# K by two transfers of 64 partitions instead of four of 32, from the ninth pack on

## The chip, the cores and the metric

The kernel runs on one NeuronCore of a Trainium2 chip. The metric is the device time of one execution in microseconds (us). Five instruction streams take part: PE (TensorE, matrix products; its weight loads are shown apart as PEld), DVE (VectorE), ACT (ScalarE), POOL (GpSimd) and SP (SyncE, which here does nothing but issue transfers). Sixteen DMA engines move the data between the device's memory and the core's on-chip memory; the transfers issued by SP go through one queue (q1 in the profile), those issued by ACT through another (q10).

## The reference

Two independent attention blocks, A and B, each with a cache of keys and values, joined along the last axis. The inputs are bfloat16 and seeded random numbers times 0.1.

```python
B, Sq, D = 16, 64, 640
H, Sk, Dh = 32, 512, 128          # k_cache, v_cache: (B, H, Sk, Dh), 64 MB each

def block(x, k_cache, v_cache, wq, wo):
    q = (x @ wq).reshape(B, Sq, H, Dh).transpose(0, 2, 1, 3)
    scores = einsum("bhqd,bhkd->bhqk", q, k_cache) * Dh ** -0.5
    p = softmax(scores, axis=-1)
    o = einsum("bhqk,bhkd->bhqd", p, v_cache)
    return o.transpose(0, 2, 1, 3).reshape(B, Sq, H * Dh) @ wo

out = concatenate([block(A...), block(B...)], axis=-1)     # (16, 64, 1280)
```

Each cache is read once. The caches are 268 MB of the 292 MB that the profile says are read.

## The kernel before, in words

**Packs.** The work is cut into 128 packs. A pack is two batches and four heads of one block; four packs (`NJ`) are a group, eight groups a phase, and there are four phases (block A heads 0-15, A 16-31, B 0-15, B 16-31). Between phases the projection weights are replaced. For a pack the kernel

- projects q for its heads (PE, `em_QP`, L611; ACT copies it out of PSUM, L617),
- turns K in 32x32 blocks (DVE, `em_KT`, L625, two instructions),
- forms the scores (PE, `em_S`, L635), takes exp with the row sums (ACT, L654), the reciprocals (DVE, L667), and multiplies (POOL, L683),
- transposes the probabilities (PE, L694; DVE copies, L704), multiplies by V (PE, `em_PV`, L717) and by the output weights (PE, `em_OP`, L737).

**Loads.** A pack needs 1 MiB of K and 1 MiB of V. `em_LDV` (L563) brings V as two transfers, one for each batch, of 128 partitions with 4 KB in each. `em_LDK` (L556) brings K as four transfers of 32 partitions with 8 KB in each. In K's tile `kn_ring` a partition is 4 * (head and eighth of the sequence) + 2 * (batch) + (half): the transfer `(n, i)` with `b = i // 2` and `l = i % 2` fills every fourth partition from `2 * b + l` on, and reads 32 pieces of 8 KB that lie 16 KB apart in the cache. The other half (`l`) is the pieces between; the other batch lies 4 MiB further on.

**Rings.** K has six buffers (`NK`), V four (`NV`). A transfer into a buffer is issued once its last reader is done: for V that is the product with V four packs earlier, on which SP waits (L571). K's transfers need no wait of their own, because SP has by then waited for something later.

**Order.** Nothing is scheduled while the kernel runs. `build_plan` (L60) gives each operation a time in units of packs (`AT`), sorts each engine's program by it, and works out from the tiles that are read and written which semaphore values have to be waited for. SP's program is the list `loads`, sorted by a due time and a class: K of a pack is due `KLEAD` = 2.5 packs ahead of V of the same pack, so that SP's queue reads: V of pack n, K of pack n + 2 or 3, V of pack n + 1, and so on, with x and the weights in between. SP's queue is taken in that order.

**Semaphores of the loads.** Each K buffer has a semaphore (`sem_key`, L268), which every finished transfer moves on. Transfers of one pack can finish in any order, so a reader waits until all of the pack are there: `PARTS` (L18) says that four make up a pack of K, and `wait_count` (L360) rounds a count up to a multiple of it; `Clocks.finish` (L341) does the same in the plan's bookkeeping of what is known to be done. The transposes L625 are the only readers of `kn_ring`. In the trace each transfer leaves, besides its data, one packet of 4 bytes on each of the 16 DMA engines, which moves the semaphore.

Of the kernel before, what the change touches and what calls it, by code (L numbers as in the profile page):

```python
# [14 lines left out]
SUM_MAX = 2.0 ** 40  # L15


PARTS = dict(d_v=2, d_k=4)  # L18


class Cfg:
    NK = 6
# [7 lines left out]
    PERIOD = 4  # L30
    BASE = 32
    KLEAD = 2.5
    NARROW = 2
    AT = dict(XT=-2.585, XE=-2.383, XC=-0.788, QP=-0.428, QE=-0.224, KT=(-0.672, -0.65), S=0,
              EX=(0.307, 0.252, 0.358, 0.4), RC=(0.45, 0.6), RCO=0.48, NM=(0.803, 0.854, 1.088, 1.187),
# [2 lines left out]


class Op:  # L40
    __slots__ = ("eng", "kind", "idx", "reads", "writes", "sem", "count", "deps", "waits", "ts", "dma")

    def __init__(self, eng, kind, idx, ts, reads=(), writes=()):
        self.eng = eng
        self.kind = kind
        self.idx = idx
        self.reads = tuple(reads)
        self.writes = tuple(writes)
        self.sem = None
        self.count = None  # L50
        self.deps = []
        self.waits = []
        self.ts = ts
        self.dma = kind in ("LDK", "LDV", "LDX", "LDWQ", "LDWO", "ST")


# [3 lines left out]
def build_plan(dims, cfg, general):  # L60
# [7 lines left out]
    AT = cfg.AT  # L68
    ops = []
    loads = []  # L70
    at = {}

    def add(eng, kind, idx, ts, reads=(), writes=()):
        op = Op(eng, kind, idx, ts, reads, writes)
        ops.append(op)
        at[(kind, idx)] = op
        return op

    def add_output(n):
# [12 lines left out]
        add("act", "OE", (n, 0), n + AT["OE"][0], [], [("B", 4), ("B", 5), ("oT", 0)])  # L92
        add("act", "OE", (n, 1), n + AT["OE"][1], [], [("B67",), ("oT", 1)])
        add("act", "ZO", n, n + AT["ZO"], [("zeros",)], [("B67",)])
        add("pe", "OP", n, n + AT["OP"], [("oT", 0), ("oT", 1), ("wo", j)], [("B67",)])
        if j == NJ - 1:
            bp = g % NBP
            add("dve", "OS", g, n + AT["OS"], [("acc", bp)], [("B67",), ("out_sb",) if final else ("acc", bp)])
            if final:
                add("act", "ST", g, n + AT["ST"], [("out_sb",)], [("out_dram", g)])  # L100
# [17 lines left out]
    for ph in range(NPH):  # L118
        twp = [ph * PH + j + (AT["WP1"] if ph else AT["WP0"]) for j in range(NJ)]
        for kt in range(dims["KT"] if ph else 0):  # L120
            ready = twp[-1] - PH + 0.5 if ph > 1 else NJ - 1 + AT["WP0"] + 0.5
            op = add("sp", "LDWQ", (ph, kt), twp[0] - 0.5, [], [("ws", kt, j) for j in range(NJ)])
# [17 lines left out]
    for n in range(-2, N):  # L140
        add_output(n)
        if n < 0:
            continue
        g, j = n // NJ, n % NJ
        add("pe", "QP", n, n + AT["QP"], [("xT", g % cfg.NX), ("wqp", j)], [("SB", 1)])
        add("act", "QE", n, n + AT["QE"], [], [("SB", 1), ("qs", n % cfg.NQ)])
        for i in range(4):
            op = add("sp", "LDK", (n, i), n + AT["KT"][0] - 0.9, [], [("kn", n % cfg.NK)])
            loads.append((n - cfg.NV + AT["PV"] + 0.2 - cfg.KLEAD, 2, op))
        for b in range(2):  # L150
            tk = n + AT["KT"][b]
            add("dve", "KT", (n, b), tk, [("kn", n % cfg.NK)], [("kt", n % cfg.NKT, b)])
        add("pe", "S", n, n + AT["S"], [("qs", n % cfg.NQ), ("kt", n % cfg.NKT, 0), ("kt", n % cfg.NKT, 1)],
            [("SB", i) for i in range(4)])
        for i in range(4):
            h = 4 * n + i
            te = n + AT["EX"][i]
            if general:
                add("dve", "MX", h, te - 0.002, [], [("SB", i), ("negmax", h % 4)])
            add("act", "EX", h, te, [("negmax", h % 4)] if general else [],  # L160
                [("SB", i), ("p", h % cfg.NP), ("rs", h)])
            add("pool" if n < N - 1 else "dve", "NM", h, n + (AT["NM"] if n < N - 1 else AT["NMZ"])[i], [("p", h % cfg.NP), ("recip", n % cfg.NR, i // 2)], [("pn", i)])
        for a in range(2):
            add("dve", "RC", (n, a), n + (AT["RCO"] if n % NJ == 1 and not a else AT["RC"][a]), [("rs", 4 * n + i) for i in (2 * a, 2 * a + 1)],
                [("recip", n % cfg.NR, a)])
# [10 lines left out]
    for op in sorted(ops, key=lambda o: o.ts):  # L176
        deps = []
# [22 lines left out]
    for k in range(reps):  # L200
        for i in range(size):
            o, o0 = pe[lo + k * size + i], pe[lo + i]
# [76 lines left out]
    for eng in ENGINES:  # L279
        for op in progs[eng]:  # L280
            op.sem = sem_key(op)
            counts[op.sem] = op.count = counts.get(op.sem, 0) + 1
    need = {}
    for op in ops:
        need[id(op)] = [e for e in (stand_in(d, op) for d in op.deps) if e is not None and e is not op]
# [39 lines left out]
class Clocks:  # L325
# [15 lines left out]
    def finish(self, eng, op):  # L341
        ck = self.clock[eng]
        self.val[op.sem] = self.val.get(op.sem, 0) + 1
        c2 = dict(ck)
        if op.dma:
            c2[op.sem] = op.count
        else:
            self.own[eng][op.sem] = op.count
            for s2, v2 in self.own[eng].items():
                if c2.get(s2, 0) < v2:  # L350
                    c2[s2] = v2
        part = PARTS.get(op.sem[0], 1)
        for k in range(op.count - 1, (op.count - 1) // part * part, -1):
            for s2, v2 in self.snap[(op.sem, k)].items():
                if c2.get(s2, 0) < v2:
                    c2[s2] = v2
        self.snap[(op.sem, op.count)] = c2


def wait_count(d):  # L360
    part = PARTS.get(d.sem[0], 1)
    return -(-d.count // part) * part


def order_waits(progs, need, base):
# [68 lines left out]
def mha_kernel(nc, blocks, out, cfg=None):  # L434
    cfg = cfg or Cfg()
# [4 lines left out]
    KT = D // 128  # L440
# [10 lines left out]
    def wide(n):  # L451
        return n < NPACK - cfg.NARROW

# [5 lines left out]
    NK, NV, NKT, NX, NXN, NQ, NP, NR = (cfg.NK, cfg.NV, cfg.NKT, cfg.NX, cfg.NXN, cfg.NQ, cfg.NP, cfg.NR)  # L459

    with contextlib.ExitStack() as es:
# [8 lines left out]
        kn_ring = sb("kn_ring", [128, NK, 2, 2048], BF16)  # L470
# [85 lines left out]
        def em_LDK(e, op):  # L556
            n, b, l = op.idx[0], op.idx[1] // 2, op.idx[1] % 2
            blk, bp, j, h = pack_info(n)
            src = blocks[blk][1][2 * bp + b, h:h + 4].rearrange("h (p l t) d -> l (h p) (t d)", l=2, t=32)[l]
            ins = e.dma_start(kn_ring[2 * b + l::4, n % NK].rearrange("p a c -> p (a c)"), src)  # L560
            return ins, ins

        def em_LDV(e, op):  # L563
# [361 lines left out]
```

## Time and profile before

| | |
|---|---|
| time, median of 3 runs | 740.34 us (740.29 to 740.70) |
| profiled execution: time / span | 740.13 us / 738.40 us |
| granted TensorE clock | 0.994 |
| PE busy | 679.2 us (92%) |
| DVE / ACT / POOL busy | 526.1 / 529.1 / 404.0 us |
| moved by DMA | 295.15 MB in 79837 packets, mean 400 GB/s |
| K transfers | 512 of 256 KB |
| V transfers | 256 of 512 KB |

The span is the time from the first to the last instruction; the profiled execution's own time is 1.73 us more, and lies 0.21 us under the median. A row of a group of instructions names the line, the engine, the operation, what is written from what, and then busy time, mean time of one, and the idle time of the engine just before them with what ended most of it. In the chain of work that ended last, an engine's name with a q (SPq) is its instruction queue: for SP that is the time that issuing a transfer took, which includes waiting until the queue has room. Rows by stage give the busy microseconds and the number of instructions of each engine in a stretch of the span, the granted clock, the mean share of the 16 DMA engines' time that packets took, and the rate. That share can exceed 1, because the records of two packets on one engine overlap slightly.

### The profile page before, as it was taken

What the parts mean: (1) busy time and instruction counts of PE and PEld (TensorE: products, weight loads), DVE (VectorE), ACT (ScalarE), POOL (GpSimd) and SP (SyncE); (2) the same over time, 40 slices, a digit from 0 to 9 for tenths busy, and PEclk for the clock granted to TensorE, in tenths of its full rate; (3) what the DMA queues carried; (4) which work ended last, traced back from release to release, by engine and by line L of the source; (5) the groups of instructions that cost most, each with busy time, mean ns of one, the idle gap of its engine ahead of it and who ended that gap; (6) DMA issues with size and microseconds to landing.
All of it is one profiled execution on the core that took longest, in us unless ns stands there. A gap on an engine that the chain in (4) does not pass through costs nothing.

```text
span 738.4 us, 61575 instructions
## 1 busy us (share of the span) xinstructions
PE 679.2 (92%) x28502; PEld 534.4 (72%) x28502; DVE 526.1 (71%) x818; ACT 529.1 (72%) x1559; POOL 404.0 (55%) x580
## 2 busy tenths in 40 slices
PE   3679999999998999989987989999999799999997
PEld 2458787787776777777766767777777577878785
DVE  7447787777757767777665677667686578788784
ACT  1448888888776767767766777777777577777775
POOL 3635555555964455554683644555577455555461
PEclk9999999999999999999999999999999999999999
DMA  9999999999999999999999999999999999999991
GB/s 323 392 404 414 415 414 414 414 414 415 409 403 413 416 416 415 416 415 415 415 402 407 414 413 415 413 414 413 416 414 402 410 415 415 416 416 417 415 371 36
DMA packets 79837, 295.15 MB, mean 400 GB/s; under 512 B 13360, under 2 KB 28208, under 8 KB 63408
## 3 DMA queue, kind: packets, MB, share of 16 engines
q1 hardware_dynamic: 68384, 281.43, 94.3%
q10 hardware_dynamic: 11408, 13.27, 5.1%
q14 instruction: 35, 0.29, 0.1%
q8 instruction: 10, 0.16, 0.1%
HBM read 292.03 MB, written 2.62 MB: 399 GB/s over the span
## 4 chain that ended last, share of the span: by engine, by line
PE 42%; SPq 40%; DMA 9%; issue 4%; POOL 2%; DVE 2%; ACT 1%; ACTq 0%; POOLq 0%; DVEq 0%
SPq L560 26%; SPq L571 12%; PE ps L717 10%; PE ps L737 10%; PE ps L611 9%; PE ps L635 8%; PE ps L694 5%; DMA kn_ring<-in_B_k_cache_dram 5%; DMA kn_ring<-in_A_k_cache_dram 2%; DMA ws_sb<-in_A_wq_dram 2%; SPq L545 1%; POOL pn_sb L683 1%; POOL wqp_sb L583 1%; DVE kt_ring L625 1%; DVE pT_sb L704 1%
## 5 line engine op out<-in xcount | busy, mean ns | idle before, releaser
L683 POOL TENSOR_SCALAR pn_sb<-p_ring,recip 128x512 bf16<-128x512 bf16 x508 | 341.8, 692 | 304.4 <-DVE recip L667 304.2
L625 DVE STREAM_TRANSPOSE kt_ring<-kn_ring 128x1024 f32<-128x1024 f32 x256 | 302.8, 1222 | 107.8 <-DMA kn_ring<-in_B_k_cache_dram 70.0
L654 ACT ACTIVATE p_ring<-ps 128x512 bf16<-128x512 f32 x512 | 297.8, 596 | 9.3 <-PE ps L635 5.6
L704 DVE COPY pT_sb<-ps 128x1024 bf16<-128x1024 bf16 x258 | 170.7, 673 | 59.9 <-PE ps L694 59.4
L717 PE MATMUL ps<-pT_sb,v_ring 32*128 32x64 bf16 x16512 | 168.0, 192 | 31.9 <-DVE pT_sb L704 17.4
L717 PEld LDWEIGHTS ps<-pT_sb,v_ring 32*128 32x128 bf16 x16512 | 151.5, 91 | 48.7 <-issue 24.8
L725 ACT ACTIVATE oT_sb<-ps 128x256 bf16<-128x256 f32 x260 | 85.6, 381 | 127.0 <-PE ps L717 127.0
L611 PE MATMUL ps<-xT_ring,wqp_sb 128*128 128x128 bf16 x2560 | 165.8, 220 | 7.3 <-POOL xT_ring L600 7.3
L611 PEld LDWEIGHTS ps<-xT_ring,wqp_sb 128*128 128x128 bf16 x2560 | 157.5, 114 | 13.6 <-issue 7.5
L737 PE MATMUL ps<-wo_sb,oT_sb 128*128 128x320 bf16 x1040 | 165.0, 302 | 1.2 <-ACT ps L729 1.2
L635 PE MATMUL ps<-kt_ring,qs_ring 32*64 32x512 bf16 x4096 | 139.7, 382 | 3.8 <-issue 3.8
L737 PEld LDWEIGHTS ps<-wo_sb,oT_sb 128*128 128x128 bf16 x1040 | 91.5, 98 | 38.2 <-ACT ps L729 1.5
L617 ACT ACTIVATE qs_ring<-ps 128x512 bf16<-128x512 f32 x128 | 76.4, 597 | 57.2 <-PE ps L611 56.5
L694 PEld LDWEIGHTS ps<-ident,pn_sb 64*128 64x128 bf16 x4128 | 68.2, 95 | 62.1 <-ACT oT_sb L725 51.9
L654 ACT ACTIVATION_READ_ACCUMULATOR p_ring<-ps 128x1 f32 x512 | 105.6, 206 | 0.0
L694 PE MATMUL ps<-ident,pn_sb 64*128 64x64 bf16 x4128 | 83.3, 191 | 8.0 <-issue 4.1
L635 PEld LDWEIGHTS ps<-kt_ring,qs_ring 32*64 32x64 bf16 x4096 | 55.2, 103 | 31.2 <-issue 5.0
L667 DVE RECIPROCAL recip<-rowsum 128x2 f32<-128x2 f32 x256 | 40.8, 159 | 37.7 <-ACT p_ring L654 29.5
L729 ACT ACTIVATE ps<-zeros 128x256 f32<-128x256 bf16 x130 | 50.4, 388 | 4.2
L583 POOL COPY wqp_sb<-ws_sb 128x1280 bf16<-128x1280 bf16 x32 | 39.2, 1254 | 15.6 <-DMA ws_sb<-in_A_wq_dram 15.6
L600 POOL COPY xT_ring<-xs_sb 128x640 bf16<-128x640 bf16 x32 | 22.9, 716 | 0.4 <-PE ps L611 0.4
L590 PE MATMUL ps<-ident,xn_ring 128*128 128x128 bf16 x165 | 14.9, 222 | 3.8 <-DMA xn_ring<-in_A_x_dram 3.2
(26 smaller groups left out, 66.0 us busy)
## 6 DMA issues: line engine op xcount, KB each, us to landing
kn_ring<-in_A_k_cache_dram SPq DMA_DIRECT2D x256, 256.0 KB
v_ring<-in_A_v_cache_dram SPq DMA_DIRECT2D x128, 512.0 KB, 14.6
kn_ring<-in_B_k_cache_dram SPq DMA_DIRECT2D x256, 256.0 KB
v_ring<-in_B_v_cache_dram SPq DMA_DIRECT2D x128, 512.0 KB, 15.5
ws_sb<-in_B_wq_dram SPq DMA_DIRECT2D x10, 512.0 KB, 16.8
wo_sb<-in_B_wo_dram ACTq DMA_DIRECT2D x8, 640.0 KB, 14.7
ws_sb<-in_A_wq_dram ACTq DMA_DIRECT2D x4, 640.0 KB, 17.7
wo_sb<-in_A_wo_dram SPq DMA_DIRECT2D x4, 640.0 KB, 14.1
```

Source lines behind the costliest of these rows:

```text
L560: ins = e.dma_start(kn_ring[2 * b + l::4, n % NK].rearrange("p a c -> p (a c)"), src)
L571: ins = e.dma_start(dst.rearrange("p t d -> p (t d)"), src.rearrange("h (p t) d -> (h p) (t d)", t=16))
L611: last = e.matmul(ps[:, 1, f * 128:(f + 1) * 128], w[:, kt, f, :], xT_ring[:, xs, kt, :], start=(kt == 0), stop=(kt == KT - 1))
L625: ins = e.transpose(dst.rearrange("p c b (h l) -> p c h b l", h=8, l=2), src)
L635: last = e.matmul(ps[64 * b:64 * b + 64, i, :], qs_ring[rows, n % NQ, f, b, :], kt_ring[rows, n % NKT, :, f // 2, b, :, f % 2], start=(f = ...
L654: ins = e.activation(dst, src, ACTF.Exp, scale=1.0, accum_out=rowsum[:, h:h + 1])
L683: ins = e.tensor_scalar(dst, src, recip[:, h // 4 % NR, i:i + 1], 1.0, ALU.mult, ALU.mult)
L694: last = e.transpose(pt_bank(b)[:, 64 * c:64 * c + 64], pn_sb[rows, c, :], ident[rows, rows], tile_position=(64 * b, 0))
L704: ins = e.tensor_copy(pT_sb[:, b].rearrange("p t q -> p (t q)"), pt_bank(b))
L717: last = e.matmul(ps[:, 4 + i, 64 * b:64 * b + 64], v_ring[rows, n % NV, b, c, :], pT_sb[rows, b, c, :], start=(t == 0 and i < 2), stop=(t ...
L725: ins = e.activation(oT_sb[:, 2 * a:2 * a + 2, :], o_ps[:, 2 * a:2 * a + 2, :], ACTF.Copy)
L737: last = e.matmul(out_ps[:, s, :], oT_sb[:, i, :], wo_sb[:, 4 * j + i, s * NH0:(s + 1) * NH0], start=(j == 0 and i == 0), stop=(j == NJ - ...
```

## The change

Packs 0 to 7 keep four K transfers. From pack 8 on there are two: transfer `l` fills every second partition from `l` on (64 partitions, 8 KB in each), and its source runs over both batches inside each piece (32 pieces, 2 batches, 4096 elements). As packs no longer have the same number of transfers, `PARTS` can't say how many make up one; each K transfer now carries the list of its pack's transfers (`group`), and the two helpers take the smallest and the largest count from that list. The transposes wait, as before, for all transfers of their pack. The order of the programs of PE, DVE, ACT and POOL and the semaphores that they wait on are the same; SP's program is the same but for 240 transfers fewer (two in each of 120 packs).

```diff
-PARTS = dict(d_v=2, d_k=4)
+PARTS = dict(d_v=2)

 class Cfg:
     KLEAD = 2.5
+    KSPLIT = 8

 # build_plan
         for i in range(4):
-            op = add("sp", "LDK", (n, i), n + AT["KT"][0] - 0.9, [], [("kn", n % cfg.NK)])
-            loads.append((n - cfg.NV + AT["PV"] + 0.2 - cfg.KLEAD, 2, op))
+            if i < 2 or n < cfg.KSPLIT:
+                op = add("sp", "LDK", (n, i), n + AT["KT"][0] - 0.9, [], [("kn", n % cfg.NK)])
+                loads.append((n - cfg.NV + AT["PV"] + 0.2 - cfg.KLEAD, 2, op))
...
+    packs = {}
+    for op in ops:
+        if op.kind == "LDK":
+            packs.setdefault(op.idx[0], []).append(op)
+            op.group = packs[op.idx[0]]

 # Clocks.finish
-        part = PARTS.get(op.sem[0], 1)
-        for k in range(op.count - 1, (op.count - 1) // part * part, -1):
+        for k in range(op.count - 1, group_start(op), -1):

+def group_start(d):
+    part = PARTS.get(d.sem[0], 1)
+    return min(o.count for o in d.group) - 1 if d.group else (d.count - 1) // part * part

 def wait_count(d):
     part = PARTS.get(d.sem[0], 1)
-    return -(-d.count // part) * part
+    return max(o.count for o in d.group) if d.group else -(-d.count // part) * part

 # em_LDK
-            src = blocks[blk][1][2 * bp + b, h:h + 4].rearrange("h (p l t) d -> l (h p) (t d)", l=2, t=32)[l]
-            ins = e.dma_start(kn_ring[2 * b + l::4, n % NK].rearrange("p a c -> p (a c)"), src)
+            src = blocks[blk][1][2 * bp:2 * bp + 2, h:h + 4].rearrange("b h (p l t) d -> l (h p) b (t d)", l=2, t=32)[l]
+            if n < cfg.KSPLIT:
+                ins = e.dma_start(kn_ring[2 * b + l::4, n % NK].rearrange("p a c -> p (a c)"), src[:, b])
+            else:
+                ins = e.dma_start(kn_ring[l::2, n % NK].rearrange("p a c -> p (a c)"), src)
```

More of the change, by code (lines that the diff above doesn't have):

```diff
@@ L40 @@
 class Op:
-    __slots__ = ("eng", "kind", "idx", "reads", "writes", "sem", "count", "deps", "waits", "ts", "dma")
+    __slots__ = ("eng", "kind", "idx", "reads", "writes", "sem", "count", "deps", "waits", "ts", "dma", "group")
     def __init__(self, eng, kind, idx, ts, reads=(), writes=()):
@@ L53, in __init__ @@
         self.ts = ts
+        self.group = None
         self.dma = kind in ("LDK", "LDV", "LDX", "LDWQ", "LDWO", "ST")
```

## The prediction, made before the changed kernel was run

> **What bounds the kernel now.** I read the page's totals first, then the rows by stage, then the chain around the last place where a transfer stands in it, and last the trace's single packet records.
>
> ```profile
> span 738.4 us, 61575 instructions
> PE 679.2 (92%) x28502; PEld 534.4 (72%) x28502; DVE 526.1 (71%) x818; ACT 529.1 (72%) x1559; POOL 404.0 (55%) x580
> ...
> DMA  9999999999999999999999999999999999999991
> ...
> DMA packets 79837, 295.15 MB, mean 400 GB/s; under 512 B 13360, under 2 KB 28208, under 8 KB 63408
> ...
> q1 hardware_dynamic: 68384, 281.43, 94.3%
> q10 hardware_dynamic: 11408, 13.27, 5.1%
> ...
> PE 42%; SPq 40%; DMA 9%; issue 4%; POOL 2%; DVE 2%; ACT 1%; ACTq 0%; POOLq 0%; DVEq 0%
> ```
>
> PE and the DMA engines are both nearly full. The chain gives 40% to SP's queue, which looks as if issuing transfers were the limit; the rows by stage say otherwise.
>
> ```profile
> core 0: us, PE busy (x) PEld busy (x) DVE busy (x) ACT busy (x) POOL busy (x), PEclk, DMA share, GB/s
> 60.00:200.00 140.00, 139.48 (x6027) 110.11 (x6012) 109.94 (x171) 114.63 (x337) 83.28 (x121) 1.00 1.02 414
> 200.00:400.00 200.00, 185.73 (x7771) 146.52 (x7768) 140.17 (x222) 143.44 (x427) 113.34 (x161) 1.00 1.03 412
> 400.00:590.00 190.00, 175.25 (x7486) 138.18 (x7488) 131.45 (x210) 137.64 (x406) 106.14 (x152) 1.00 1.02 413
> 590.00:712.00 122.00, 121.73 (x5119) 96.21 (x5112) 96.59 (x148) 94.27 (x281) 65.90 (x99) 1.00 1.02 415
> 712.00:738.00 26.00, 20.89 (x843) 15.98 (x840) 15.62 (x32) 15.04 (x46) 8.04 (x12) 0.96 0.32 121
> ```
>
> The DMA engines are full up to 712 us. PE is full from 60 to 200 us and from 590 to 712 us, but between, it stands idle for 14.27 + 14.75 = 29.0 us. So the middle is bound by the DMA engines; before and after it PE sets the pace, with the DMA engines only just keeping up. What PE lacks in the middle is K:
>
> ```profile
> DVE kt_ring L625 <- DMA kn_ring<-in_B_k_cache_dram: 70.0, 53, 3.8
> DVE kt_ring L625 <- DMA kn_ring<-in_A_k_cache_dram: 37.6, 30, 3.0
> ...
> 569.75 18.86 DMA kn_ring<-in_B_k_cache_dram
> 588.61 0.02 issue
> 588.64 2.37 DVE kt_ring L625 x2
> ```
>
> The last two transposes that the chain reaches through a transfer start at 588.64 us; they are those of pack 102 (the 205th and 206th). From there the chain to the end is PE and its evacuations. So the kernel ends sooner by what the transfers up to K of pack 102 gain; what later ones gain, PE hides.
>
> **What a transfer costs a DMA engine.** SP issues 802 transfers and ACT 33; 835 x 16 = 13360, exactly the packets under 512 B: each transfer ends in one 4-byte packet per engine. The packet records of q1 give its length: median 9 ns, against 313 ns for an 8 KB packet (K) and 160 ns for a 4 KB packet (V). The records also tell what it costs. Over 100 to 180 us, where one data packet follows another directly its record starts 3 or 4 ns (mean 3.6) before the earlier one ends; where a 4-byte packet lies between, it starts 2 or 3 ns (mean 2.4) after. So a completion takes 2.4 + 3.6 = 6.0 ns of its engine. With 3.55 ns taken off each record the engines are full in every 10 us from 10 to 710 us, so there is nothing else to gain between packets. [...]
>
> **The change part by part.**
>
> *Completions removed.* Two transfers less in each of the 95 packs 8 to 102 are 190 completions on each engine: 190 x 6.0 ns = 1.14 us. Bounds: 0 if they hide behind the next packet after all; 190 x 9 ns = 1.71 us if the record's whole length counts. I take 1.14. The remaining 25 packs remove another 50 x 6.0 = 0.30 us behind PE's last stage: nothing.
>
> *K's packets themselves.* Pieces, their 8 KB, and the partitions that each sixteenth of a pack's rows covers stay the same. New is that neighbours in a transfer alternate between the batches, 4 MiB apart, instead of lying 16 KB apart. The nearest rows (100 to 180 us): the second packet of a K transfer, 16 KB behind the first, takes 312.9 ns on average; the first behind another K transfer 312.6 (one in three of these has made the 4 MiB jump to the other batch, the rest a step of 8 KB); the first behind V, in another tensor, 314.2. So I bound a jump by -0.3 and +1.3 ns; with 95 packs x 8 packets per engine = 760 packets that is -0.2 to +1.0 us. I take 0, since the row nearest to it, which holds such jumps within the cache, shows no cost.
>
> *SP's queue.* 240 issues fewer at a median of 0.595 to 0.600 us are 143 us less of SP's time. In the middle SP is held up by a full queue; elsewhere it waits for V's buffers (75.2 us on the products with V). As the engines never run empty, an earlier issue only lengthens the queue: 0. V, x and the weights behind K move up, with the same result. If that cover went (engines running dry between SP's issues), each pack would gain up to 1.2 us; no 10 us stretch in the middle shows it. Bounds: 0, and SP's shorter program may save one or two of the 8 KB instruction fetches (q14, about 315 ns each, on one engine): 0.6 us.
>
> *The transposes' wait.* They waited for four transfers and now wait for two, all of the pack both times; no reader used a quarter. The last byte comes at the same place in the queue: 0. Queued behind L625 on DVE are the reciprocals and copies of the packs in flight, as before. Waits of PE, ACT and POOL, and ACT's own transfers, are unchanged: 0.
>
> *The first eight packs* keep their transfers: 0.
>
> Sum: -1.14 us. The profiled execution took 740.13 us (span 738.40 and 1.73 around it), which would become 738.99; it lies 0.21 us below the median, so against 740.34 I predict **739.2 us**. What a measurement here can tell from no change is about 0.2%, 1.5 us: below 738.86 is faster, above 741.82 slower. The forecast falls just short of that line.
>
> **Rivals.**
>
> *Larger gain.* All bounds at their good ends: 1.71 + 0.2 + 0.6 = 2.5 us, 737.8; at half way 738.3. For it: the engines are full and every term has the same sign. Against: the records' measured 6.0 ns.
>
> *No gain.* The completions hide, or K's packets at +1.3 ns eat the gain (+1.0 - 1.14): 740.2 to 740.3. Against: the 2.4 ns gap behind each completion.
>
> *Slower: K's packets grow by the alternation of batches.* Place: the 8 KB packets of packs 8 to 102. A packet of this size has a floor at 309 ns, and its values spread to some 320, so there is something in the memory's answer that varies. If alternation moved the mean by 5 ns, from 313 to 318, within that spread, 760 x 5 = 3.8 us, less 1.14: +2.7, 743.0. It eats the gain from 1.5 ns on and reads as slower from (1.14 + 1.48) / 760 = 3.4 ns on. Against: the jump rows above. [...]
>
> [...]
>
> *The change doesn't do what it says:* the issuing hardware cuts the three-dimensional source into 4 KB packets. Two 4 KB packets take 2 x 162.7 ns, less 3.6 overlap, 321.8 against 313.4: 760 x 8.4 = 6.4 us, less 1.14: 745.6. Against: a piece is still one run of 8 KB on both sides.
>
> *SP's issuing is the limit after all,* as the chain's 40% reads. Then PE's idle 29.0 us in the middle would go: 711. Against it: the engines are full, and faster issuing can't make them move more.
>
> **How the numbers follow.** Forecast 0.43; larger gain 0.25; no gain 0.12; slower by alternation 0.14; doubled packets 0.01; cut packets 0.03; SP's issuing 0.02. The forecast's own spread is about that of the runs (740.29 to 740.70) and of the packets' jitter, some 0.6 us, so that a quarter of it (0.11) falls below 738.86. Faster: 0.11 + 0.25 + 0.02 = 0.38; within: 0.32 + 0.12 = 0.44; slower: 0.14 + 0.01 + 0.03 = 0.18. Range: from 737.6, under the larger gain's end by the runs' spread, to 742.0, past the line for slower; it leaves out most of the alternation's case and the three rare ones, under 2 in 10. The forecast's own range is 738.5 to 739.9.
>
> **What would show it.** Packets under 512 B: 13360 - 3840 = 9520, with the packets from 8 KB up unchanged in number (79837 - 63408 = 16429); if that number falls, K was cut. The mean of the 8 KB packets from pack 8 on, near 313 ns: the term on which all hangs. PE idle 27.9 us instead of 29.0 between 200 and 590 us; the last transfer in the chain near 587.5 us; the stage behind it still nearly all PE. SP's K issues at 240 fewer, with longer ones among them, since the queue is as full as before. I am wrong if the 8 KB packets change length by more than 1 ns, if engines come to stand idle before 710 us, or if a stage that is now PE's gets waits on transfers.

## The result, and the profile after

| | before | after |
|---|---|---|
| time, median of 18 runs each | 740.35 us (739.64 to 741.11) | 739.09 us (738.82 to 740.18) |
| ratio after / before, 95% interval | | 0.9985 [0.9979, 0.9991] |
| profiled execution: time / span | 740.13 / 738.40 us | 739.09 / 737.31 us |

The change saves 1.26 us (1.55 to 0.67 by the interval), 0.15%: just inside the 0.2% that was set as the line for "no change". The forecast was 739.2 us.

The page of the kernel after, its totals, its DMA queues and its chain:

```profile
span 737.3 us, 61335 instructions
PE 678.4 (92%) x28502; PEld 531.3 (72%) x28502; DVE 521.8 (71%) x818; ACT 529.6 (72%) x1559; POOL 404.0 (55%) x580
...
DMA packets 75995, 295.12 MB, mean 400 GB/s; under 512 B 9520, under 2 KB 24368, under 8 KB 59568
...
q1 hardware_dynamic: 64544, 281.41, 94.4%
...
PE 47%; DMA 25%; SPq 12%; DVE 5%; POOL 4%; issue 3%; ACT 2%; ACTq 0%; POOLq 0%; DVEq 0%
```

The transfers did what the diff says: 9520 packets under 512 B, as many as forecast, and 75995 - 59568 = 16427 of 8 KB and more (16429 before; a few records can be missing), so K was not cut. The bytes are the same. In the chain, SP's issuing fell from 40% to 12%, and the transfers themselves rose from 9% to 25%. The time hardly moved: the 40% were no cost of issuing that fewer issues would save. K's issues, fewer by 240, took 1.01 us each on average instead of 0.79.

The rows by stage of the kernel after (us, busy time and count of each engine, granted clock, DMA share, GB/s):

```profile
60.00:200.00 140.00, 139.47 (x6071) 110.00 (x6060) 110.45 (x171) 114.42 (x336) 83.22 (x121) 1.00 1.02 414
200.00:400.00 200.00, 187.18 (x7790) 146.58 (x7782) 140.39 (x223) 144.07 (x428) 114.55 (x162) 0.99 1.02 412
400.00:590.00 190.00, 176.36 (x7501) 137.97 (x7499) 131.47 (x208) 139.07 (x409) 105.64 (x152) 0.99 1.02 413
590.00:712.00 122.00, 119.78 (x5135) 94.66 (x5136) 93.47 (x149) 94.31 (x283) 66.95 (x100) 1.00 1.02 416
```

The DMA share and the rate are those of before (414, 412, 413, 415). In the middle PE is idle for 12.82 + 13.64 = 26.5 us, 2.6 us less. In the last row something is new: PE has 2.22 us of idle time, where before it had 0.27.

The chain of the kernel after, from 560 us on (start, length, what):

```profile
566.29 21.95 DMA kn_ring<-in_B_k_cache_dram
588.26 2.37 DVE kt_ring L640 x2
...
632.08 18.44 DMA kn_ring<-in_B_k_cache_dram
650.55 2.38 DVE kt_ring L640 x2
...
669.05 18.19 DMA kn_ring<-in_B_k_cache_dram
687.26 2.37 DVE kt_ring L640 x2
```

Before, the last transfer in the chain ended at 588.6 us. Now K still decides at 588.3, 650.6 and 687.3 us. And SP now waits longer for V's buffers (us in total, times, longest). Before:

```profile
SPq L571 <- PE ps L717: 75.2, 56, 4.4
```

After:

```profile
SPq L586 <- PE ps L732: 166.1, 87, 4.8
```

**Where the 1.09 us of the profiled pair lie.** Three things can be measured in the two traces.

*The rate.* From 60 to 590 us the kernel before moved 218.688 MB and the kernel after 218.737 MB: 0.05 MB more, 0.12 us at 413 GB/s. (From the start to 590 us it is 241.237 and 241.294 MB, 0.14 us.) The completions that were removed had taken 190 x 6.0 ns = 1.14 us of each engine up to there. The reason stands in the packets: the 8 KB packets became longer, 313.72 to 314.45 ns from 60 to 200 us, 314.14 to 314.82 up to 400, 314.43 to 315.35 up to 590, and V's 4 KB packets too (162.70 to 163.02, 162.40 to 162.81, 162.71 to 162.94), though nothing about V was changed. A pack gives an engine 8 of the one and 16 of the other on average: about 8 x 0.7 + 16 x 0.3 = 10.4 ns, against the 12 ns that two completions took. What was freed between the packets, the packets took back.

*K's arrival.* The transposes of pack 43 start 0.13 us earlier than before, those of pack 102 0.37 us, those of pack 127 0.40 us. From pack 35 or so on the transposes start within 0.1 us of the last completion of their K in both kernels, in all but a few packs, so this is the DMA engines' own pace. Single executions differ by as much: in the variants below whose medians lie within 0.6 us of the kernel after (one V transfer, two or six idle instructions on SP, two K transfers from the start), the transposes of pack 102 start between 0.70 us earlier and 0.45 us later than before. So the 0.37 us can't be put down to the change.

*PE's last stage.* From the transposes of pack 127 to the end it is 20.1 us before and 19.4 us after: 0.7 us. This part comes back in single executions: it is 19.4 or 19.5 us in seven of the eight variants below that have three or four transfers for a pack, and 18.8 us in the eighth (twelve idle instructions on SP). In the kernel before, PE had fallen behind here. The products with V are 128 matmuls in a row, and the groups of that line between 590 and 712 us differ in busy time at nearly the same count. Before:

```profile
L717 PE MATMUL ps<-pT_sb,v_ring 32*128 32x64 bf16 x2944 | 30.7, 192 | 0.3 <-DVE out_sb L750 0.3
```

After:

```profile
L732 PE MATMUL ps<-pT_sb,v_ring 32*128 32x64 bf16 x2964 | 28.2, 192 | 2.2 <-DVE out_sb L765 1.4 <-DVE pT_sb L719 0.6
```

30.7 us / 2944 is 10.4 ns for each, 28.2 / 2964 is 9.5. One run of 128 takes 1.21 or 1.22 us in the kernel after, each time; before, it takes 1.22 to 1.57 there. The records show the difference: in the kernel before, single gaps of 35 ns and more (up to 195) stand inside the runs, 24 from 590 us to the end, together 2.1 us. None lies among the first 60 products of a run. In the kernel after there is no gap. So before, PE was full to the end and slower, and it ended 0.7 us behind K; after, PE keeps up, and the transposes wait for K longer. The group of the transposes from 590 to 712 us, before and after:

```profile
L625 DVE STREAM_TRANSPOSE kt_ring<-kn_ring 128x1024 f32<-128x1024 f32 x47 | 55.7, 1222 | 5.0 <-DMA kn_ring<-in_B_k_cache_dram 4.9
L640 DVE STREAM_TRANSPOSE kt_ring<-kn_ring 128x1024 f32<-128x1024 f32 x47 | 55.8, 1224 | 21.8 <-DMA kn_ring<-in_B_k_cache_dram 21.8
```

PE's own 2.2 us of idle time there are mostly ended by DVE's copies (`out_sb`, `pT_sb`), which stand between the transposes in DVE's program. What PE waits for in a gap no view names. The instruction fetches on record (queues q8 and q14) don't account for it: from 590 to 712 us there are five before and four after, against 24 gaps and none. Whether the gaps go with the number of transfers is taken up with the small packets below.

How much of the 1.26 us is the change's own is less certain than its interval says. Five variants below keep the change's transfers or have fewer, and differ in little else (V by one, in all packs but the last two or from the ninth on; two or six idle instructions on SP; two K transfers from the start). Four of them came out at ratios of 0.9989 to 0.9993 to the kernel before, 0.5 to 0.8 us under it, and the fifth at 1.0001. The 0.7 us of PE's last stage alone would fit the four.

### The profile page after: what moved, and what is told of

The parts are those of the page before. It is cut to its first block, busy times and chain, and to the rows that moved or that the text cites. A ratio compares the mean times of both kernels' runs of the same rounds, so it can differ in the third digit from the quotient of the medians.

```text
span 737.3 us, 61335 instructions
## 1 busy us (share of the span) xinstructions
PE 678.4 (92%) x28502; PEld 531.3 (72%) x28502; DVE 521.8 (71%) x818; ACT 529.6 (72%) x1559; POOL 404.0 (55%) x580
## 2 busy tenths in 40 slices
DMA packets 75995, 295.12 MB, mean 400 GB/s; under 512 B 9520, under 2 KB 24368, under 8 KB 59568
## 4 chain that ended last, share of the span: by engine, by line
PE 47%; DMA 25%; SPq 12%; DVE 5%; POOL 4%; issue 3%; ACT 2%; ACTq 0%; POOLq 0%; DVEq 0%
DMA kn_ring<-in_B_k_cache_dram 15%; PE ps L732 13%; PE ps L752 11%; PE ps L626 10%; PE ps L650 8%; DMA kn_ring<-in_A_k_cache_dram 8%; SPq L586 6%; PE ps L709 5%; SPq L575 5%; DVE kt_ring L640 3%; DMA ws_sb<-in_A_wq_dram 2%; POOL pn_sb L698 2%; POOL wqp_sb L598 2%; DVE pT_sb L719 2%; ACT p_ring L669 1%
## 5 line engine op out<-in xcount | busy, mean ns | idle before, releaser
L732 PE MATMUL ps<-pT_sb,v_ring 32*128 32x64 bf16 x16512 | 163.3, 192 | 30.9 <-DVE pT_sb L719 15.5
L732 PEld LDWEIGHTS ps<-pT_sb,v_ring 32*128 32x128 bf16 x16512 | 148.5, 91 | 46.5 <-issue 26.2
L752 PE MATMUL ps<-wo_sb,oT_sb 128*128 128x320 bf16 x1040 | 166.8, 304 | 1.7 <-ACT ps L744 1.6
L650 PEld LDWEIGHTS ps<-kt_ring,qs_ring 32*64 32x64 bf16 x4096 | 53.1, 103 | 31.9 <-issue 4.4
```

What stands on the lines that cost most here:

```text
L650: last = e.matmul(ps[64 * b:64 * b + 64, i, :], qs_ring[rows, n % NQ, f, b, :], kt_ring[rows, n % NKT, :, f // 2, b, :, f % 2], start=(f = ...
L732: last = e.matmul(ps[:, 4 + i, 64 * b:64 * b + 64], v_ring[rows, n % NV, b, c, :], pT_sb[rows, b, c, :], start=(t == 0 and i < 2), stop=(t ...
L752: last = e.matmul(out_ps[:, s, :], oT_sb[:, i, :], wo_sb[:, 4 * j + i, s * NH0:(s + 1) * NH0], start=(j == 0 and i == 0), stop=(j == NJ - ...
```

## The experiments

All kernels below start from the kernel after, compute the whole output, and are compared with the kernel before. Two theories run through the expectations. By the first, that of the prediction, each completion taken away gives its time on the engines back. By the second the removed completions gave nothing, and the gain has to do with the DMA engine that finishes last: it supposes that this engine also fetches instructions for an instruction queue, which has less to fetch when SP's program is shorter (35 packets on q14 before, 33 after).

**Four transfers of 32 partitions, but with alternating batches.** It was to test the alternation of batches without the smaller number of transfers.

```diff
-            if i < 2 or n < cfg.KSPLIT:
-                op = add("sp", "LDK", ...)
+            op = add("sp", "LDK", ...)
...
-                ins = e.dma_start(kn_ring[l::2, n % NK]..., src)
+                ins = e.dma_start(kn_ring[64 * b + l:64 * b + 64:2, n % NK]..., src[16 * b:16 * b + 16])
```

> Four K transfers of 32 partitions per pack again, but each now alternates between the two batches (upper and lower half of the partitions instead of one batch each): the alternation of the change without its smaller count. Theory 1 (what counts is completions, 6.0 ns of every DMA engine for each transfer): the gain is gone, 740.2 to 740.5 us, as before. Rival (what helped is the source that runs over both batches): 739.1 as in the changed kernel. Rival (alternation costs something that the smaller count outweighs): above 740.8.

Measured: 1085.92 us, in runs that lay between 882.71 and 1134.57, against 740.2. All expectations missed by far; why single runs lie so far apart isn't shown. The page of one of 1092.2 us:

```profile
DMA packets 79836, 295.15 MB, mean 271 GB/s; under 512 B 13360, under 2 KB 28208, under 8 KB 63408
```

The packets are as before in number and size, but the 8 KB packets take 498 ns on average and V's 4 KB packets 220. Two things were changed at once here: each transfer also lies within one half of the partitions (0 to 63, or 64 to 127). The next run says which it is.

**V by four transfers of 64 neighbouring partitions.** It was to double V's completions and leave K alone.

```diff
-PARTS = dict(d_v=2)
+PARTS = dict(d_v=4)
...
+            rows = slice(64 * (op.idx[1] % 2), 64 * (op.idx[1] % 2) + 64)
...
-            dst = v_ring[:, n % NV, b]
+            dst = v_ring[rows, n % NV, b]
```

> The changed kernel, but V comes by four transfers of 64 partitions in a pack instead of two of 128, so that a pack has six transfers as before the change, and no packet of K or V has another size or source. Theory 1: 256 completions more on each engine, 95 to 120 packs of them in front of the last K that is waited for, so 1.1 to 1.4 us more than 739.1: 740.2 to 740.5. Rival (K's shape and not the count): 739.1.

Measured: 1191.21 us, ratio 1.5959 [1.5923, 1.5995]. Missed again. The page:

```profile
span 1184.6 us, 61595 instructions
...
GB/s 307 270 280 266 255 253 251 248 244 250 268 258 269 266 258 252 251 253 247 253 253 254 245 245 244 236 238 240 238 240 256 249 246 247 246 245 246 251 250 99
DMA packets 80092, 295.15 MB, mean 249 GB/s; under 512 B 13616, under 2 KB 28464, under 8 KB 63664
```

No batch alternates in these transfers, and the rate falls as in the run above: 8 KB packets 509 ns, 4 KB packets 272. What the two kernels have in common is a transfer that stays within 64 neighbouring partitions, and a mean rate of 271 and 249 GB/s against 400. The change's own transfers also have 64 partitions, but every second one of all 128, and keep 413 GB/s. Why the choice of the partitions matters no run here shows. So the alternation of batches was not tested by itself. In the change it comes with transfers that reach over all 128 partitions and with packets 0.7 ns longer.

**V by one transfer for both batches.** 126 transfers fewer again, of V this time, so 126 completions on each engine.

```diff
...
-        for b in range(2):
+        one = 0 <= n < N - cfg.NARROW
+        for b in range(1 if one else 2):
...
+                both = blocks[blk][2][2 * bp:2 * bp + 2, h:h + 4].rearrange("b h (p t) d -> (h p) b (t d)", t=16)
+                ins = e.dma_start(v_ring[:, n % NV].rearrange("p b t d -> p b (t d)"), both)
```

> The changed kernel, but V comes by one transfer over both batches in a pack instead of two, in packs 0 to 125: three transfers in a pack. Theory 1: 126 completions fewer on each engine, 0.6 to 0.75 us less than 739.1: 738.4. Rival (the gain was K's alone): 739.1. Rival (larger transfers make the wait for V's buffers or for the last half of V dearer): above 739.5.

Measured: 739.48 us (738.93 to 740.24), ratio 0.9993 [0.9984, 1.0001]. Packets under 512 B fell to 7504, and there is no further gain. The first packs lost some: 22.39 MB were moved by 60 us instead of 22.55 MB, 0.4 us. From 60 to 590 us it moved 218.788 MB, 0.05 MB more than the kernel after: 0.12 us for some 100 packs whose one completion of 6 ns should have given 0.6. The first theory fails here as it did for K.

**Twelve idle instructions for each pack on SP.** SP's program becomes longer (1440 semaphore additions that nobody reads), the transfers stay.

```diff
+        s_nil = es.enter_context(nc.semaphore("s_nil"))
...
+            if p == 0 and op.kind == "LDV" and op.idx[1] == 0 and op.idx[0] >= 8:
+                for _ in range(12):
+                    e.sem_inc(s_nil, 1)
```

> The changed kernel with twelve more instructions in SP's program in each pack from pack 8 on, each of which only adds one to a semaphore that nobody reads: 1440 instructions more, the same transfers. Theory 1: the transfers' completions alone made the gain, so nothing changes, 739.1. Theory 2: part of the gain is that SP's program has 240 instructions fewer, which one DMA engine has to fetch in 8 KB packets (33 in place of 35 packets in the profile after), and the last of the sixteen engines decides when a pack of K is there. Then some 11 more fetches of 0.32 us on that engine give up to 3.6 us more: 741 to 742.7.

Measured: 742.47 us, ratio 1.0031 [1.0019, 1.0043], 3.4 us more than the kernel after. The rate in the middle is unchanged (414, 412, 413 GB/s). The queue that fetches instructions:

```profile
q14 instruction: 45, 0.37, 0.1%
```

There are 12 more of its 8 KB packets (33 in the kernel after; 1440 / 12 = 120 instructions each). SP has time to spare (in the kernel after it waits 166.1 us for V's buffers), so the second theory lived on: the change had removed 240 SP instructions, two such packets.

**Two and six idle instructions for each pack on SP.** Two give SP's program back exactly what the change took away (240). The diff is that of two; six stand in packs 8 to 125, ahead of V's transfers.

```diff
+        s_nil = es.enter_context(nc.semaphore("s_nil"))
...
+            if p == 0 and op.kind == "LDK" and op.idx[1] == 0 and op.idx[0] >= 8:
+                for _ in range(2):
+                    e.sem_inc(s_nil, 1)
```

> The changed kernel with two idle instructions in SP's program in each pack from pack 8 on, so that SP's program is as long as before the change (240 more), with the transfers of the changed kernel. Theory 1 (completions alone): 739.1. Theory 2 (what the last DMA engine has to fetch): 240 / 128 = 1.9 fetches of 0.32 us, 0.6 us more, 739.7, half of the gain gone. If the whole gain were instructions: 740.2 to 740.4.

> The changed kernel with six idle SP instructions in each of packs 8 to 125 (708 more), as the partner of the next run, which has six transfers more there. Theory 2, by the slope of e4 (3.4 us for 1440): 1.7 us more than 739.1, 740.8. Theory 1: 739.1.

Measured: two, 739.22 us, ratio 0.9992 [0.9983, 1.0001]; six, 739.37 us, ratio 0.9992 [0.9983, 1.0001]. Beside the change's 0.9985 [0.9979, 0.9991] neither can be told from no effect, and the 740.8 us expected for six were missed. The effect is 0.1 and 0.3 us by the medians and 0.5 us by the ratios, so these runs don't rule out that SP's shorter program made a part of the gain, the 0.6 us of the second theory included. They do show that the cost is no straight line: 708 instructions cost no more than 240 by the ratios, and 1440 cost 3.4 us. That fits an engine which has some room until it becomes the last.

**V by eight transfers over every fourth partition.** It was to have many completions without the halves of the partitions.

```diff
-PARTS = dict(d_v=2)
+PARTS = dict(d_v=8)
...
+            if many:
+                ins = e.dma_start(v_ring[r::4, n % NV, b].rearrange("p t d -> p (t d)"),
+                                  src.rearrange("h (p t) d -> (h p) (t d)", t=16)[r::4])
```

> The changed kernel, but V of packs 8 to 125 comes by eight transfers in a pack, each over every fourth partition, instead of two: 708 completions more on each engine; SP's program is 780 instructions longer, 72 more than in e6. [...] Theory 1: 6.0 ns for each completion in front of the last K, 3.4 to 4.2 us more than e6: 744.3 to 745.2 if e6 is at 740.8. Theory 2 with a common limit (data packets become shorter by what completions take, since the sixteen engines share some 415 GB/s, so completions cost nothing): within 0.5 us of e6, 740.8 to 741.3. Rival: SP's issuing becomes the limit (two K at 0.6 us and eight V at 0.43 to 0.58 us are 4.6 to 5.8 us in a pack of 5.2): above 750, with engines idle in the middle.

Measured: 878.11 us, ratio 1.1866 [1.184, 1.1893]. SP's queue from 400 us on (start, length, what):

```profile
400.47 5.30 SPq L587 DMA_DIRECT2D v_ring<-in_A_v_cache_dram  x8
405.81 1.24 SPq L575 DMA_DIRECT2D kn_ring<-in_A_k_cache_dram  x2
407.10 5.47 SPq L587 DMA_DIRECT2D v_ring<-in_A_v_cache_dram  x8
```

Here SP never waits: it issues without a break, at 5.30 / 8 = 0.66 us and 1.24 / 2 = 0.62 us from one issue to the next, and ten of them take 6.6 us where a pack takes 5.2 us otherwise. In the whole run it waits 3.5 us for V's buffers. This is what an issue-bound queue looks like:

```profile
200.00:400.00 200.00, 170.11 (x6617) 129.73 (x6618) 114.33 (x185) 119.20 (x355) 94.87 (x135) 0.94 0.95 342
```

The DMA share falls to 0.95 and the rate to 342 GB/s. The share falls so little because the packets' records are longer here: 374 ns for 8 KB and 175 for 4 KB on average, instead of 315 and 163. In the two runs with 64 neighbouring partitions the share is even 1.01 and 1.03 from 60 to 590 us, at 275 and 257 GB/s. So the share alone does not tell that the engines move what they can. The kernel before, with six issues for each pack, 413 GB/s and 75.2 us in which SP waits for V's buffers, was not issue-bound, whatever its chain's 40% said.

**Twelve, and four, idle instructions for each pack on ACT.** The same as on SP, on ACT. The diff is that of twelve.

```diff
+        s_nil = es.enter_context(nc.semaphore("s_nil"))
...
+            if p == 0 and op.kind == "OE" and op.idx[1] == 0 and op.idx[0] >= 8:
+                for _ in range(12):
+                    e.sem_inc(s_nil, 1)
```

> The changed kernel with twelve idle instructions in ACT's program in each pack from pack 8 on, ahead of the copy of the output out of PSUM, where ACT stands waiting for PE about 1 us in each pack. If ACT's program is fetched by the same DMA engine as SP's: 11 fetches of 0.32 us, 742.5, as in e4. If by another engine that is not the last: 739.1 to 739.4. If the instructions themselves hold ACT up: more than 743, with PE idle in the stages where it is now full.

> The changed kernel with four idle instructions in ACT's program in each pack from pack 8 on (480 more, 3.75 fetches of 8 KB), a third of e8, which lay 6.8 to 7.0 us over the changed kernel. If the engine that fetches for ACT is the last of the sixteen all along, and a fetch costs it what e8 gives, 0.6 us: 2.3 us more, 741.4. If a fetch costs the 0.32 us of its packet's record: 1.2 us more, 740.3. If e8 was slow because ACT itself was held up, a third of it would hide in ACT's idle time: 739.1.

Measured: twelve, 745.92 us, ratio 1.008 [1.0067, 1.0093]; four, 741.88 us, ratio 1.0029 [1.0019, 1.0039]. With twelve, the instruction queue:

```profile
q14 instruction: 46, 0.37, 0.1%
```

The waits of the transposes (us in total, times, longest):

```profile
DVE kt_ring L640 <- DMA kn_ring<-in_B_k_cache_dram: 99.1, 63, 3.5
DVE kt_ring L640 <- DMA kn_ring<-in_A_k_cache_dram: 42.4, 30, 2.9
```

In the kernel after:

```profile
DVE kt_ring L640 <- DMA kn_ring<-in_B_k_cache_dram: 85.3, 61, 3.6
DVE kt_ring L640 <- DMA kn_ring<-in_A_k_cache_dram: 37.1, 29, 2.9
```

141.5 us of waiting for K instead of 122.4, at 412 GB/s from 200 to 590 us as against 412 and 413: the sixteen engines together move as much as before, but K comes later. The reason is in the completions of one pack. Each transfer of K has 16, and the transposes start within 0.1 us of the last of them. The 32 completions of pack 127 with twelve instructions on ACT, after the first issue: 30 of them by 9.07 us, and the last two at 17.92 and 19.17 us. In the kernel before, the last completions lie 2.1 us behind the median for packs 24 to 31, and 8.2 us behind for packs 120 to 127 (after: 1.9 and 7.8). The traces don't name the engine of a packet; that the late completions are all of one engine, that it is the one which fetches ACT's program, in 8 KB packets of about 316 ns, and that it falls behind a little at each one, is inferred. With twelve on ACT they are 12.9 us behind for packs 120 to 127, with four 10.0, with twelve on SP 11.2, with six on SP 8.5. Along the run with twelve the transposes' lateness goes up in steps of about 0.6 us. Over the whole it is 6.8 us for 46 - 33 = 13 more fetches, 0.5 us each; with four, 2.8 us for 37 - 33 = 4, 0.7 us each (by the medians). If ACT's engine is the last all along, and SP's program is fetched by another, it starts to cost at once, without the room that SP's engine has; the four costs fit that. The record of a fetch shows about half of that cost, 0.32 us; the other half stays open.

**V by one transfer, later, at the same length of SP's program.** The second transfer of a pack gives way to an addition of 16 to its semaphore; the first eight packs keep two.

```diff
+            one = cfg.KSPLIT <= n and wide(n)
-            if n < 0:
+            if n < 0 or one and b:
```

> The changed kernel, but V comes by one transfer over both batches in each of packs 8 to 125 only (in e3 also in packs 0 to 7, where 0.16 MB less had been moved by 60 us, 0.4 us). In the place of the second transfer SP adds 16 to the semaphore itself, so its program is as long as before. Theory 1 (6.0 ns of each engine for each completion): 95 to 118 completions fewer, 0.6 to 0.7 us less than the changed kernel: 738.4 or a ratio to the kernel before near 0.9976. Theory 2 (the engines share a limit, the data packets lengthen by what the completions took): no less than the changed kernel, ratio 0.9985.

Measured: 739.2 us, ratio 0.9989 [0.998, 0.9998]. No further gain, without the loss at the start: fewer completions are worth nothing from here on. From 60 to 590 us it moved 218.744 MB (218.737 in the kernel after).

**Three small transfers more in each pack.** 16 rows of 4 bytes each into a tile that nobody reads: 11328 packets under 512 B more, and little data.

```diff
+        s_nil = es.enter_context(nc.semaphore("s_nil"))
...
+            if p == 0 and op.kind == "LDK" and op.idx[1] == 0 and 8 <= op.idx[0] < 126:
+                for i in range(3):
+                    t = 3 * (op.idx[0] - 8) + i
+                    e.dma_start(spare[t % 8::8, t // 8 * 2:t // 8 * 2 + 2], blocks[0][0][0, 0:16, 0:2]).then_inc(s_nil, 16)
```

> The changed kernel with three more transfers in each of packs 8 to 125, each of 16 rows of 4 bytes from x into unused room, one row for each engine, that nobody waits for: on each engine 354 data packets of 4 bytes and 354 completions more, with SP's program 354 instructions longer (e6 showed 708 to cost 0.1 to 0.5 us). Theory 1: at 6 ns for each of the two packets, 285 x 12 ns = 3.4 us to K of pack 102, 4.2 us in all, over the changed kernel: 742.5 to 743.3. Theory 2 (small packets are paid out of the slack of a shared limit): under 1 us over the changed kernel.

Measured: 745.32 us, ratio 1.0074 [1.006, 1.0088], 6.2 us more than the kernel after by the medians. The page and two of its rows by stage:

```profile
DMA packets 87326, 295.19 MB, mean 397 GB/s; under 512 B 20848, under 2 KB 35696, under 8 KB 70896
```

```profile
200.00:400.00 200.00, 189.45 (x7967) 148.60 (x7965) 141.54 (x223) 146.37 (x435) 118.73 (x166) 0.99 1.03 409
400.00:590.00 190.00, 174.50 (x7319) 137.25 (x7318) 132.27 (x211) 137.64 (x406) 104.42 (x149) 0.99 1.03 410
```

The rate falls by 3 GB/s in each stage. By 590 us 239.967 MB were moved instead of 241.294, 3.2 us' worth, for some 600 more small packets on each engine by then: 5.4 ns each, near the 6.0 ns that the prediction read from the records. So small packets do cost their time when they are added, and gave nothing back when they were taken away. Both hold if the rate of the data itself has an upper bound at 413 to 416 GB/s in these stages, which the kernel before just touched. All kernels here with three to six transfers for a pack, those with 64 neighbours aside, moved 412.6 to 412.8 GB/s from 60 to 590 us. What sets such a bound no run shows.

The rest of the loss lies behind 590 us, where PE is full (121.78 of 122 us). The transposes of pack 102 start 3.2 us later than in the kernel after, those of pack 127 5.0 us, and from there to the end it is 20.2 us instead of 19.4. The group of the products with V between 590 and 712 us:

```profile
L733 PE MATMUL ps<-pT_sb,v_ring 32*128 32x64 bf16 x2944 | 32.8, 192 | 0.2
```

11.1 ns for each, against 9.5 in the kernel after. From 590 us to the end 34 gaps of 35 ns and more (up to 221) stand inside the runs of 128 products, 4.1 us together, and from 60 to 200 us, where PE is full in every kernel of the table but the first, 21 with 2.2 us. Here too none lies among the first 60 products of a run. In both stages the kernel after has none. The counts for these two stages, in kernels by the number of transfers for a pack:

| kernel | transfers of K, V and the small ones in a pack | gaps 60-200 us | gaps 590 us to the end |
|---|---|---|---|
| V by eight | 10 | 29 (3.3 us) | 29 up to 712 us (3.3 us) |
| small transfers added | 7 | 21 (2.2 us) | 34 (4.1 us) |
| before | 6 | 1 (0.1 us) | 24 (2.1 us) |
| after | 4 | 0 | 0 |
| twelve on SP / twelve on ACT | 4 | 0 / 0 | 1 / 2 (0.1 us) |
| two, six on SP; four on ACT | 4 | 0 | 0 |
| V by one; V by one, later | 3 | 0 | 0 |

Added transfers bring gaps in these stages: the kernel of the second row is the one of the fourth with nothing but these transfers added. But their number is not all. The kernel before has one gap from 60 to 200 us and 24 in the last stage, with six transfers in both. The two kernels with 64 neighbours, six transfers at a lower rate, have 32 and 9 gaps from 60 to 200 us and none and 34 from 590 to 712. And from 200 to 590 us, where PE has time to spare, the kernels of the table, V by eight aside, have 26 to 66 gaps, also those with three or four transfers. By which way a transfer holds PE up was not tried.

**Two K transfers from the first pack on.**

```diff
-    KSPLIT = 8
+    KSPLIT = 0
```

> The changed kernel with two K transfers in all packs, the first eight too. Theory 1: 16 completions fewer, 0.1 us less, which can't be told from no change: 739.0 to 739.1. Rival (the first packs are waited for piece by piece, and larger transfers put the first V and weights behind more of K): 0.3 to 1 us slower than the changed kernel.

Measured: 739.61 us, ratio 1.0001 [0.9992, 1.0011]: by the ratios the gain of the change is gone. The first 60 us:

```profile
0.00:60.00 60.00, 32.89 (x1112) 24.64 (x1113) 29.74 (x37) 22.21 (x60) 24.65 (x34) 0.91 0.99 377
```

In the kernel after:

```profile
0.00:60.00 60.00, 35.87 (x1245) 27.21 (x1246) 31.35 (x39) 23.59 (x64) 26.64 (x38) 0.97 0.99 377
```

The rate is the same, PE has done 3.0 us less work, and the transposes of packs 8 to 29 start 2.8 to 2.9 us later than in the kernel before (0.7 to 0.9 in the kernel after). That the first eight packs' larger transfers did this isn't shown: the granted clock is 0.91 in this row and 0.97 in that of the kernel after, and the run with two idle instructions on SP, which has four K transfers in these packs, starts packs 8 to 29 later than before by 2.2 to 2.4 us, at a clock of 0.86. The middle, which waits for the DMA engines anyway, takes most of the delay back: pack 64 starts 0.3 us and pack 127 0.1 us later than before. By the medians 0.4 us of the gain are left (739.61 against 739.99); three of the eleven runs, at 740.89 to 742.78, weigh on the ratio.

## Why the prediction was right in its total, and where its steps were not

**Removed completions, 1.14 us: mis-sized.** The 190 completions did go (9520 packets), and the 6.0 ns for each was near what added packets cost (5.4 ns). But the freed time did not become throughput: 0.12 to 0.14 us of the 1.14. The step from "the engines are full" to "what is freed is gained" failed, because the data packets stretched. "No gain", one of the rivals, is what happened to the rate, by its own mechanism in part: K's packets grew by 0.7 ns on average, within the +1.3 ns that it allowed. It did not see V's 4 KB packets grow as well, which speaks against the alternation alone.

**K's packets, 0 between -0.3 and +1.3 ns: the bounds held,** the taken value was low by 0.7 ns (0.7 to 0.9 by stage). No run separates the alternation from the rest of that. The traces hold a packet's queue, time and size, but neither its address nor its engine: which packets of the prediction's rows had made a jump, and that it is the memory's answer that varies between 309 and 320 ns, were the author's reading.

**"From pack 102 on PE hides everything": failed.** PE is full there before (121.73 of 122 us) only since 2.1 us of gaps stand in its products with V. In the kernel after the gaps are gone, PE has 2.22 us to spare, and K decides at 650.6 and 687.3 us too: a stage that was PE's got waits on transfers, one of the signs of being wrong that the prediction named. The 0.7 us between K of the last pack and the end is the larger part of the profiled pair's gain, and the prediction's sum has no term for it; 1.14 us of the wrong term happened to stand where 0.4 us of earlier K and 0.7 us of PE's last stage stood. That the total came out within 0.1 us is thus luck and no proof of the sum.

**SP's queue, 0: right.** Its waits for V's buffers rose from 75.2 to 166.1 us, K's issues became fewer and longer (from 0.79 to 1.01 us on average), the rate stayed at 413 GB/s. No view names what a long issue waits for; that it is room in the queue was the author's reading. The longest issue of K took 3.7 us before and 3.8 after, but 0.68 us from the ninth pack on with eight V transfers, where SP doesn't wait. The rival that SP's issuing was the limit would have shown as in the run with eight V transfers, with the DMA share at 0.95.

**SP's shorter program, 0 to 0.6 us: not told from 0.** Two instructions for each pack given back gave 0.9992 [0.9983, 1.0001] beside 0.9985 [0.9979, 0.9991]; 0.6 us isn't ruled out either. No trace shows that the fetches fall on one engine, as that bound takes it, and no run shows the 128 instructions for a fetch by which the expectations got 1.9 and 3.75 fetches: counted were 2 fewer with 240 instructions fewer, and 4 more with 480 on ACT, 12 more with 1440 on SP and 13 more with 1440 on ACT, so 111 to 120 instructions each.

**The transposes' wait, 0, and K not cut: right.** PE's idle time in the middle was forecast at 27.9 us and is 26.5. The last transfer in the chain, forecast near 587.5 us, is at 687.3.

**The other rivals.** "Slower by alternation" needed 3.4 ns for each packet, and there were 0.7. Doubled or cut packets did not come: 16427 of 8 KB and more, against 16429.

## What to carry to other kernels

A share of 1.0 on the DMA engines (1.02 from 60 to 590 us here, before and after) says that packets fill their time, not that a shorter packet list moves more bytes: look whether the data packets' own length gives way (here 8 KB packets by 0.7 to 0.9 ns), and test from both sides, with packets added and packets taken away. Before a transfer is split or merged, see which partitions each part reaches: every second of all 128 kept 413 GB/s from 60 to 590 us here, 64 neighbours 275 and 257, about a third less. The share of time alone hides that: it stood at 1.01 and 1.03 there. When a stage is called bound by an engine because it is full, compare what one of its instructions takes there with the same instruction elsewhere (10.4 ns before and 9.5 after, in the products with V); part of that busy time may be a stall that a change removes, as the gaps of 2.1 us in the last stage were here.

## What the runs showed that was not expected

- Transfers within 64 neighbouring partitions: 249 and 271 GB/s instead of 400, with 8 KB packets of 498 to 509 ns instead of 315.
- Idle instructions cost time, and K comes later: with twelve for each pack on ACT the transposes wait 141.5 us for it, 122.4 in the kernel after. On ACT, 1440 of them cost 6.8 us and 480 cost 2.8 us; on SP, 708 cost some tenths at most and 1440 cost 3.4 us. The engines that run them had time to spare. The last completions of K's packs 120 to 127 come 7.8 us behind the median in the kernel after, 12.9 with 1440 on ACT and 11.2 with 1440 on SP; that they are those of the one DMA engine which fetches the program is inferred.
- Added packets of a few bytes cost 5.4 ns each; the 3840 that the change took away gave back a tenth of their time in rate.
- Ten issues of 32 or 64 spread partitions take SP 6.6 us, 0.6 to 0.7 us each: more than a pack's 5.2 us.
- PE's products with V stall inside a run of 128: in the last stage 4.1 us with seven transfers for a pack, 2.1 with six and next to none with four or three. Where PE was full the stalls lay behind the 60th product of a run. From 200 to 590 us, where PE has time to spare, it also stalls with four or three. Open is what PE waits for in these gaps.
